# Sliding-window attention and an ELU feed-forward layer on one core: the casts on POOL in four to six instructions each instead of one

## The chip, the cores and the metric

The kernel runs on one core of one Trainium2 chip. The core has five engines that take their instructions in program order from their own queues and meet through semaphores: PE (matrix multiply, with its weight loads shown apart as PEld), DVE (vector), ACT (scalar, activation functions), POOL (GpSimd) and SP (issues transfers). SP, ACT and POOL issue DMA transfers. The metric is the time of one execution on the device in microseconds (us). The kernel before was timed seven times: median 341.12 us, lowest 340.13, highest 346.49.

## What is computed

Eight batches of eight heads, 576 positions, 64 channels per head. Each position attends to positions at most 32 away; the result of all heads (4608 tokens by 512) goes through a layer of 512 to 2048 and back with an ELU between.

```python
# _attn_ref, cut
scores = scale * np.matmul(q, k.transpose(0, 1, 3, 2))
mask = np.abs(pos[:, None] - pos[None, :]) <= 32
scores = np.where(mask, scores, -1000000000.0)
attn = softmax(scores)
attn_out = np.matmul(attn, v)              # (8, 8, 576, 64)
# _moe_ref
x = attn_out.transpose(0, 2, 1, 3).reshape(4608, 512)
h = x @ w_in                               # 512 -> 2048
g = np.where(h > 0.0, h, np.exp(np.minimum(h, 0.0)) - 1.0)
out = g @ w_out                            # 2048 -> 512
```

## The kernel before

**Inputs q and k.** They arrive as fp32 in four loads a batch: q and k, each in two halves of four heads (`load_qk`, L228), into one of four `stg` buffers. A cast (`cast`) turns each half into bf16 in a `bf` tile, of which there are four (q and k of two batches). PE then transposes the `bf` tile, one pair of heads `hp` at a time (`T`, L264 and L269), into PSUM, and ACT or DVE copies the result to `qT` or `kT` (`E`, L281 and L283).

There are two layouts. Batches 0 and 1 are "wide": 128 partitions, and a half is 2 x 576 = 1152 columns (`wide`, `TPW` = 9, `D` = 64). Batches 2 to 7 are "narrow": 96 partitions, and a half is 4 heads x 6 positions x 64 channels = 1536 columns (`HP` = 4, `TPP` = 6). Batch 0 is cast by DVE and ACT (`casts0`), batches 1 to 7 by POOL: 4 wide casts (L244) and 24 narrow ones (L252), in the order k, q, k, q, each when its load has landed.

**Attention.** For each pair `i` of blocks of 64 queries (36 pairs): scores on PE (`QK`, L327), exp on ACT (`SM`, L335) into `pu`, the mask multiplied in by two DVE instructions (`MK`, L348: `pm` = `pu` times `masks`, all three in SBUF), the product with v on PE (`AV`, L360), reciprocal and scaling on DVE (`RN`, L373 and L375) into `xs`. Then `xs` is transposed into `xt`: for the first eight pairs by PE and ACT, and for the others by a transposing transfer that SP issues (`X`, L386).

**Feed-forward.** The tokens are worked on in tiles of 256 (the first two) and 512 (the other eight). For each of 16 column groups `fo` of a tile: four matmuls into `psH` (`Hm`, L407, three buffers), exp on ACT into `e` (`EX`, L415), min(e - 1, 0) into `f`, on DVE (`FF`, L427: input `e` fp32 in SBUF, output bf16 in SBUF) or on ACT (L425), and the ELU on DVE from `psH` and `f` (`GG`, L433 or L436). The second product (`Y`, L450) runs a tile later, in parts between the `Hm` groups; ACT copies it out of PSUM (`YC`, L460) and SP stores it.

**Loads of v and of the weights.** POOL issues them (L291, L492, L497), in its queue between its casts. For batches 2 and up, SP then issues two copies that shift v by 64 partitions (`shift_v`, L298 and L300), in its queue between the stores and the transposing transfers.

**Order.** A planner written in the kernel (`Plan`) simulates the engines with an estimated duration, a rank and dependencies per operation, and issues the operations in the order of that simulation. A cast is one operation for it (`cdur`, 1.5 us on POOL, times 0.78 for a wide one). The queues are therefore fixed at build time, and a framework puts in the semaphore waits according to what each instruction reads and writes.

Of the kernel before, what the change touches and what calls it, by code (L numbers as in the profile page):

```python
# [150 lines left out]
def kernel(  # L151
# [9 lines left out]
    nc = tc.nc  # L161

    B, H, S, D = q.shape
# [7 lines left out]
    HP = H // 2  # L171
    PR = 96
    TPP = S // PR
    TPW = S // QB
# [41 lines left out]
    def wide(b):  # L216
        return b < NWB
# [13 lines left out]
    def cast(b, nm, half, eng):  # L231
        if (nm, b) not in live:
            live[nm, b] = bfp.tile(
                [128, HP, TPW, D] if wide(b) else [PR, TPP, H, D], BF16,
                name="bf", tag="bf")
        t = live[nm, b]
        if wide(b):
            src = live.pop((nm, b, half))
            dst = t[:, half * HP // 2:(half + 1) * HP // 2].rearrange(
                "p n t d -> p n (t d)")  # L240
            if eng is nc.scalar:
                nc.scalar.copy(dst, src)
            else:
                eng.tensor_copy(dst, src)  # L244
            return
        src = live.pop((nm, b, half)).rearrange("p h (t d) -> p h t d", t=TPP)
        dst = t[:, :, half * HP:(half + 1) * HP, :].rearrange(
            "p t h d -> p h t d")
        if eng is nc.scalar:
            nc.scalar.copy(dst, src)  # L250
        else:
            eng.tensor_copy(dst, src)  # L252

    def T(b, nm, hp):
        src = live[nm, b]
# [269 lines left out]
    for b in range(B):  # L525
# [4 lines left out]
        for half in range(2):  # L530
            for nm in ("q", "k"):
                deps = list(early)
                if b == 1:
                    deps.append(("SM", L1AT))
                if b == 2:
                    deps.append(("LV", 1, 8))
                if b:
                    deps.append(("C", b - 1, nm, half))
                P.op(("L", b, nm, half), "ACT" if b or nm == "q" else "SP", 0.45,
                     r0 + half, deps,  # L540
                     lambda b=b, nm=nm, half=half: load_qk(
                         b, nm, half,
                         nc.scalar if b or nm == "q" else nc.sync),
                     dma=1.6 if wide(b) else 1.85, wt=0.085, solo=0.75)
                eng = casts0[nm, half] if b == 0 else "POOL"
                deps = [("L", b, nm, half)]
                if b >= 2:
                    deps += [("T", b - 2, nm, hp) for hp in range(HP)]
                P.op(("C", b, nm, half), eng,
                     cdur[eng] * (0.78 if wide(b) else 1.0), need - 30 + half, deps,  # L550
                     lambda b=b, nm=nm, half=half, eng=eng:
                     cast(b, nm, half, engs[eng]))
# [30 lines left out]
        for hp in range(HP):  # L583
            for nm in ("q", "k"):
                n = hp * 2 + (nm == "k")
                deps = [("C", b, nm, hp // 2)]
                m = n - (4 if b == 0 else 1)
# [20 lines left out]
    for i in range(NPAIR):  # L608
# [15 lines left out]
        t, c = where[i]  # L624
# [81 lines left out]
    with tc.manual_schedule():  # L706
# [3 lines left out]
        for mi in range(3):  # L710
            m = mf[:, mi, :]
# [6 lines left out]
        for lo, key in ((0, QB), (QB, 0)):  # L718
            m = mf[lo:lo + QB, 3, :]
# [54 lines left out]
```

## Time and profile before

| what | value |
|---|---|
| median of 7 runs | 341.12 us |
| the profiled execution | 340.55 us, of which 338.8 are the span from its first to its last instruction |
| granted PE clock | full throughout |
| L427, `f` on DVE, 128x512 | 92 instructions, mean 497 ns, median 0.42 us |
| L348, mask on DVE, 128x512 | 72 instructions, mean 510 ns, median 0.418 us |
| L252, narrow cast on POOL | 24 instructions, 1.463 to 1.681 us |
| L244, wide cast on POOL | 4 instructions, 1.143 to 1.147 us |

A page of the profile gives busy time by engine, the chain of work that ended last followed back from the end, and the costliest groups of instructions with the idle time ahead of them and what ended it. The trace can be asked for a timeline of an engine in a stretch, for the chain in order of time, and for a table of busy time by stretches. All positions are in us from the start of the span. In a timeline a row gives the start, the duration, the engine, the line, the operation and the tiles, and in square brackets how long the engine was idle before and what ended that.

The 28 casts on POOL come in seven groups of four: at 26 to 37 us (wide), and at 55 to 64, 87 to 97, 115 to 125, 152 to 162, 185 to 194 and 219 to 227 us (narrow). In all groups but the first and the last, five v loads follow the fourth cast on POOL's queue without a break.

### The profile page before, as it was taken

The page shows a single profiled execution, that of the slowest core. Times are in us where ns is not written, and L with a number is a line of the kernel's source. Part 1 is how long each engine was busy: PE and PEld are TensorE (multiplying, and loading weights), DVE is VectorE, ACT ScalarE, POOL GpSimd, SP SyncE. Part 2 cuts the span into 40 slices and gives each one's busy share as a digit, 9 for nine tenths or more (in the row PEclk, how much of TensorE's full clock was granted, in tenths as well). Part 3 has the DMA queues.
Part 4 walks back from the last instruction along what each step waited for, and adds up shares of the span by engine and source line. Part 5 has one row for each costly group of instructions (what it writes and reads, how often), then busy time and mean ns, then how long its engine had stood idle before and what let it go on. Part 6 is the DMA issues. An engine that isn't in the chain of part 4 may idle for free.

```text
span 338.8 us, 7578 instructions
## 1 busy us (share of the span) xinstructions
PE 312.1 (92%) x2995; PEld 170.2 (50%) x3040; DVE 233.3 (69%) x522; ACT 207.6 (61%) x355; POOL 84.2 (25%) x96
## 2 busy tenths in 40 slices
PE   1589998799889998999999999999999999999995
PEld 1576666554444545545554555455544544444442
DVE  5778888648966796669757976697666777655500
ACT  3558868677877566655865576567655565444511
POOL 8916503800470262005501630150000000000000
PEclk9999999999999999999999999999999999999999
DMA  7999999892999889259996893684111112200021
GB/s 278 180 238 292 191 121 258 151 89 75 236 123 109 223 158 168 67 132 243 99 130 161 214 141 86 167 207 106 52 49 46 48 46 61 64 34 31 31 92 65
DMA packets 77364, 44.58 MB, mean 132 GB/s; under 512 B 54161, under 2 KB 70801, under 8 KB 77329
## 3 DMA queue, kind: packets, MB, share of 16 engines
q0 software_dynamic: 41728, 8.92, 35.0%
q1 hardware_dynamic: 24224, 17.36, 21.1%
q10 hardware_dynamic: 11376, 17.83, 20.9%
q8 instruction: 24, 0.39, 0.5%
q14 instruction: 12, 0.09, 0.1%
HBM read 36.70 MB, written 9.44 MB: 136 GB/s over the span
## 4 chain that ended last, share of the span: by engine, by line
PE 76%; DMA 8%; DVE 7%; ACT 4%; issue 2%; ACTq 1%; POOL 0%; SPq 0%; POOLq 0%
PE psH L407 32%; PE psY L450 29%; PE psO L360 4%; PE psT L269 3%; DMA stg<-in_q_dram 3%; PE psS L327 3%; DMA xt<-xs 3%; DMA stg<-in_k_dram 2%; DVE f L427 2%; DVE g L436 2%; DVE xs L375 1%; ACT e L415 1%; PE psO L450 1%; PE psS L450 1%; PE psT L450 1%
## 5 line engine op out<-in xcount | busy, mean ns | idle before, releaser
L407 PE MATMUL psH<-xt,w_in_sb 128*128 128x512 bf16 (+1 forms) x624 | 146.0, 359 | 3.6 <-DVE g L436 1.5
L415 ACT ACTIVATE e<-psH 128x512 f32<-128x512 f32 (+1 forms) x160 | 87.7, 555 | 87.2 <-PE psH L407 77.2
L450 PE MATMUL psY<-w_out_sb,g 128*128 128x512 bf16 x499 | 128.3, 379 | 2.9 <-issue 1.6
L407 PEld LDWEIGHTS <-w_in_sb 128*128 128x128 bf16 x640 | 59.1, 98 | 56.8 <-issue 4.1
L450 PEld LDWEIGHTS <-g 128*128 128x128 bf16 x576 | 52.3, 98 | 54.3 <-issue 0.9
L427 DVE TENSOR_SCALAR f<-e 128x512 bf16<-128x512 f32 (+1 forms) x108 | 54.0, 500 | 31.8 <-ACT e L415 31.7
L436 DVE TENSOR_TENSOR g<-psH,f 128x512 bf16<-128x512 f32 (+1 forms) x108 | 70.3, 651 | 3.3
L252 POOL CAST bf<-stg 96x1536 bf16<-96x1536 f32 x24 | 35.6, 1484 | 127.6 <-DMA stg<-in_k_dram 116.0
L433 DVE SCALAR_TENSOR_TENSOR g<-f,psH 128x512 bf16<-128x512 bf16 (+1 forms) x52 | 31.2, 601 | 22.2 <-ACT f L425 22.0
L335 ACT ACTIVATE pu<-psS 128x1024 bf16<-128x1024 f32 x36 | 36.8, 1023 | 4.8 <-PE psS L327 3.9
L348 DVE TENSOR_TENSOR pm<-pu,masks 128x512 bf16<-128x512 bf16 x72 | 33.7, 510 | 3.7 <-ACT pu L335 3.4
L291 POOL DMA_DIRECT2D vw<-in_v_dram x40 | 34.2, 869 | 5.1 <-DMA w_out_sb<-in_moe_w_out_dram 2.7
L360 PEld LDWEIGHTS <-pm 128*128 128x128 bf16 x576 | 26.9, 101 | 14.3 <-DVE xs L375 1.7
L375 DVE TENSOR_TENSOR xs<-psO,rc 128x256 bf16<-128x256 f32 x68 | 28.9, 424 | 2.3
L360 PE MATMUL psO<-vw,pm 128*128 128x65 bf16 x544 | 29.1, 196 | 1.3 <-DVE xs L375 0.7
L425 ACT ACTIVATE f<-e 128x512 bf16<-128x512 f32 (+1 forms) x52 | 29.4, 566 | 1.4
L373 DVE RECIPROCAL rc<-psO 128x4 f32<-128x4 f32 x68 | 12.2, 179 | 20.7 <-PE psO L360 20.0
L281 ACT COPY qT<-psT 128x576 bf16<-128x576 bf16 x30 | 19.1, 637 | 8.2 <-PE psT L269 6.5
L269 PEld LDWEIGHTS <-bf 96*128 96x128 bf16 x288 | 17.1, 98 | 11.5 <-issue 1.8
L460 ACT COPY y<-psY 128x512 f32<-128x512 f32 x33 | 18.9, 573 | 5.4 <-remote 4.3
L269 PE MATMUL psT<-ident,bf 96*128 96x96 bf16 x288 | 20.2, 206 | 1.9 <-ACT kT L281 0.8
L281 ACT COPY kT<-psT 128x576 bf16<-128x576 bf16 x28 | 17.8, 636 | 6.0 <-PE psT L269 5.4
(48 smaller groups left out, 107.4 us busy)
## 6 DMA issues: line engine op xcount, KB each, us to landing
stg<-in_q_dram ACTq DMA_DIRECT2D x16, 576.0 KB, 10.1
out_dram<-y SPq DMA_DIRECT2D x35, 256.0 KB, 3.3
stg<-in_k_dram ACTq DMA_DIRECT2D x14, 576.0 KB, 8.4
vw<-vw SPq DMA_DIRECT2D x12, 260.0 KB, 6.0
vw<-in_v_dram POOLq DMA_DIRECT2D x24, 128.0 KB, 6.5
w_in_sb<-in_moe_w_in_dram POOLq DMA_DIRECT2D x4, 512.0 KB, 9.3
w_out_sb<-in_moe_w_out_dram POOLq DMA_DIRECT2D x4, 512.0 KB, 22.3
vw<-in_v_dram POOLq DMA_DIRECT2D x16, 96.0 KB, 6.3
```

Of the source, the lines that this page charges most:

```text
L252: eng.tensor_copy(dst, src)
L269: nc.tensor.transpose(pt[:, j, :], src[:, j, 2 * hp:2 * hp + 2, :], ident[0:PR, 0:PR])
L281: nc.scalar.copy(dst, src)
L291: nc.gpsimd.dma_start(out=vt[r:r + hi - lo, qb, :, 0:D], in_=vb[lo:hi])
L335: nc.scalar.activation(pu, live.pop(("S", i)), AX.Exp, scale=SCALE)
L348: nc.vector.tensor_mul(dst, pu[:, :, s], mb)
L360: nc.tensor.matmul(o[:, j, :], lhsT=p[:, h, s * QB:s * QB + 128], rhs=vw[b % NVB][:, qb, h, :], start=(s == 0), stop=(s == 1))
L407: nc.tensor.matmul(ps, lhsT=w_in_sb[:, do, fo * 128:(fo + 1) * 128], rhs=xts[t][:, do, :], start=(do == 0), stop=(do == NDO - 1))
L415: nc.scalar.activation(e, ps, AX.Exp)
L427: nc.vector.tensor_scalar(f, e, -1.0, 0.0, ALU.add, ALU.min)
L436: nc.vector.tensor_tensor(gs[t][:, fo, :], ps, f, ALU.max)
L450: nc.tensor.matmul(ps, lhsT=gs[t][:, fo, c * 128:(c + 1) * 128], rhs=w_out_sb[:, fo, :], start=(fo == 0), stop=(fo == NFO - 1))
```

## The change

`cast` issues several instructions where it issued one. A wide cast on POOL becomes six of 128x192 (two head pairs by three column groups of 192); a narrow one becomes four of 96x384, one per head. What is read, what is written and the arithmetic stay the same.

```diff
@@ def cast @@
             if eng is nc.scalar:
                 nc.scalar.copy(dst, src)
+            elif eng is nc.gpsimd:
+                m = TPW * D // 3
+                for n in range(HP // 2):
+                    for c in range(0, TPW * D, m):
+                        eng.tensor_copy(dst[:, n, c:c + m], src[:, n, c:c + m])
             else:
                 eng.tensor_copy(dst, src)
             return
         src = live.pop((nm, b, half)).rearrange("p h (t d) -> p h t d", t=TPP)
         dst = t[:, :, half * HP:(half + 1) * HP, :].rearrange(
             "p t h d -> p h t d")
-        if eng is nc.scalar:
-            nc.scalar.copy(dst, src)
-        else:
-            eng.tensor_copy(dst, src)
+        for j in range(HP):
+            eng.tensor_copy(dst[:, j], src[:, j])
```

The planner's numbers are untouched, so no operation changes its place in any queue. On POOL the 28 casts become 4 x 6 + 24 x 4 = 120 instructions; PE, DVE, ACT and SP issue the same instructions in the same order as before. The first piece of a cast carries the wait for the load; the others have none. A transpose on PE now waits for the pieces that it reads: a narrow `T` reads two heads, so two of the four pieces, and a wide one reads three of the six, each a wait of its own.

## Prediction

> **What bounds the kernel now.** I read the page first: engine shares, then the chain that ended last, then the group of the casts.
>
> ```profile
> PE 312.1 (92%) x2995; PEld 170.2 (50%) x3040; DVE 233.3 (69%) x522; ACT 207.6 (61%) x355; POOL 84.2 (25%) x96
> PE 76%; DMA 8%; DVE 7%; ACT 4%; issue 2%; ACTq 1%; POOL 0%; SPq 0%; POOLq 0%
> L252 POOL CAST bf<-stg 96x1536 bf16<-96x1536 f32 x24 | 35.6, 1484 | 127.6 <-DMA stg<-in_k_dram 116.0 <-DMA stg<-in_q_dram 11.0 <-PE psH L407 0.6
> ```
>
> PE carries the end. POOL has almost nothing of the chain and idles 127.6 us ahead of its casts, so the length of a cast as such is not what costs. What could cost is what a cast does to another engine. The timeline of POOL and of DVE, side by side, shows it:
>
> ```profile
> 115.44 1.46 POOL L252 CAST bf<-stg 96x1536 bf16<-96x1536 f32 x1 [14.73 <-DMA stg<-in_k_dram]
> 117.75 1.46 POOL L252 CAST bf<-stg 96x1536 bf16<-96x1536 f32 x1 [0.85 <-DMA stg<-in_q_dram]
> 120.69 1.52 POOL L252 CAST bf<-stg 96x1536 bf16<-96x1536 f32 x1 [1.48 <-DMA stg<-in_k_dram]
> 123.48 1.46 POOL L252 CAST bf<-stg 96x1536 bf16<-96x1536 f32 x1 [1.27 <-DMA stg<-in_q_dram]
> ```
>
> ```profile
> 115.84 1.35 DVE L427 TENSOR_SCALAR f<-e 128x512 bf16<-128x512 f32 x1
> 118.38 1.12 DVE L427 TENSOR_SCALAR f<-e 128x512 bf16<-128x512 f32 x1
> 120.14 0.75 DVE L348 TENSOR_TENSOR pm<-pu,masks 128x512 bf16<-128x512 bf16 x2
> 121.41 1.09 DVE L427 TENSOR_SCALAR f<-e 128x512 bf16<-128x512 f32 x1
> 123.56 1.67 DVE L427 TENSOR_SCALAR f<-e 128x512 bf16<-128x512 f32 x1
> ```
>
> Columns are start and duration. L427 takes 0.42 where no cast runs. Here each one that starts inside a cast ends 0.29 after that cast ends (115.44 + 1.46 = 116.90, against 117.19), so it stood still until about 0.13 before the cast's recorded end. L348 is stretched likewise: a pair takes 0.75 alone, and 1.29, 1.56, 1.85, 1.71 and 1.71 from 88.08, 89.89, 154.03, 187.33 and 220.91. L436 and L433 never are (maxima 0.693 and 0.689). Over the run, the excess of L427 and L348 during casts sums to some 16 us of DVE time.
>
> Does it reach the end? The table by stretches (span, then busy us of PE, PEld, DVE, ACT, POOL):
>
> ```profile
> 86.00:99.00 13.00, 10.71 (x107) 5.65 (x108) 10.79 (x24) 9.68 (x16) 8.49 (x7) 1.00 0.98 170
> 114.00:132.00 18.00, 16.40 (x174) 8.83 (x176) 15.84 (x31) 11.21 (x17) 10.04 (x9) 1.00 1.17 183
> 132.00:230.00 98.00, 96.46 (x869) 50.82 (x883) 71.93 (x149) 62.95 (x105) 26.05 (x22) 1.00 0.82 150
> 230.00:330.00 100.00, 99.00 (x673) 48.14 (x683) 61.13 (x131) 53.35 (x89) 0.00 (x0) 1.00 0.18 55
> ```
>
> From 132 to 230 there are 12 casts, yet PE idles only 1.54 of 98 us. The cast-free 100 us after that show 1.00. There the DVE waits are covered by PE's own queue. Ahead of 132 it differs. In the chain in order of time, the links from 114.68 to 126.53 are all DVE, and end in a transfer that PE waits for:
>
> ```profile
> 115.92 1.28 DVE f L427
> ...
> 118.46 1.04 DVE f L427
> ...
> 123.64 1.60 DVE f L427
> ...
> 126.53 4.69 DMA xt<-xs
> ```
>
> PE's timeline gives what can be won there:
>
> ```profile
> 120.28 1.02 PE L407 MATMUL psH<-xt,w_in_sb 128*128 128x512 bf16 x4 [0.29 <-DVE g L436]
> 126.89 0.72 PE L360 MATMUL psO<-vw,pm 128*128 128x65 bf16 x8 [0.27 <-DVE pm L348]
> 129.01 0.42 PE L360 MATMUL psO<-vw,pm 128*128 128x65 bf16 x8 [0.28 <-DVE xs L375]
> 131.36 0.81 PE L407 MATMUL psH<-xt,w_in_sb 128*128 128x512 bf16 x3 [0.36 <-DMA xt<-xs]
> ```
>
> With 0.16 more at 116.00 (that gap recurs where no cast is) these are 1.36 us, of which 1.20 hang on DVE.
>
> **The change, part by part: the pieces.** 24 casts of 96x1536 become 96 of 96x384, and 4 of 128x1152 become 24 of 128x192. No such piece is in the trace. Three rows give a line: POOL's cast into masks, 256 columns, 0.396; 1152 columns, 1.146; 1536 columns, 1.463. That is 0.18 fixed and 0.837 ns a column, so 0.50 for 384 and 0.34 for 192. Independent neighbours on POOL overlap a little: the affine selects at 2.00 and 2.18 are 0.18 apart at 0.24 each, so I take 0.06 off per step. A narrow cast is then 4 x 0.44 + 0.06 = 1.82 (from 1.46), a wide one 6 x 0.28 + 0.06 = 1.74 (from 1.15). Bounds: no fixed cost at all leaves 1.46 and 1.15; 0.396 scaled by columns (0.594) or unscaled gives 2.38 for both.
>
> **What the longer casts delay.** (a) Transposes on PE (L264, L269). They wait for the pieces they read, half a narrow cast instead of all of it. In the whole trace PE waits for L252 at one place, 0.9 us at 59.49. The smallest other slack of a first transpose is that of 92.32 against a q cast ended at 90.84, 1.48 us, while half a cast is done 0.94 after its start. Cost nothing; without that cover about 0.4 at each of five batches. (b) POOL's queue behind the casts: the v loads (L291). They start 0.4 to 1.5 later. The first four casts are each followed by idle of POOL (0.87, 0.92, 1.76 and, at the ring of loads, 1.49) that absorbs 0.59 apiece. (c) SP's shift copies (L298) wait for those loads, with stores and transposing transfers queued behind. SP waited for a v load once, 0.6 us at 56.7, and the next transposing transfer starts at 70.64. Cost nothing. (d) The next batch's loads wait for the casts to free stg: the last ends at 63.88, the next load is issued at 81.79. Nothing.
>
> **What the shorter pieces free.** The disputed point is whether a waiting DVE instruction gets in between two pieces. No two casts are back to back in this trace. The nearest rows are trains of load issues on POOL, which hold DVE up as well: L427 at 127.08 took 0.59 and ended at 127.67, inside a train from 124.89 to 129.07, and the one at 99.70 took 0.49 inside 96.53 to 100.71. Both went ahead with the next POOL instruction queued. So I take "gets in", after 0.22 on average (half a 0.44 step), 0.44 at most.
>
> The Trainium skill, GPSIMD Engine Reference, section Instruction dispatch, speaks against this: consecutive Pool instructions are no barrier, and a core begins the next one once its own share is done. By it a train of pieces might never leave a hole, and the sum would be that of the second rival below, by the rows the one here; no run here shows which holds for casts.
>
> By stage:
> - 28 to 31: L427 at 29.24 took 1.09 against 0.28, behind a wide cast. It would wait 0.13, but PE's transposes at 30.23 need three pieces, ready at about the same time. Gain 0.2 of 0.60 idle.
> - 57 to 60: the q cast started at 57.97 on a landing load. Two pieces and one DVE instruction of 0.28 between them: 57.97 + 0.94 + 0.28 = 59.19 against 59.43. Gain 0.25, at most 0.5.
> - 86 to 99: excess 0.54 and 0.81 in two L348 pairs. A pair asks twice and can meet a piece each time, 0.22 + 0.44 = 0.66, so the first pair gains nothing. Of PE's idle 2.15 only 0.87 were ended by DVE or xt. Gain 0.4, between 0 and 1.35.
> - 114 to 132: the four L427 lose 0.93 + 0.70 + 0.67 + 1.25 = 3.55; with pieces 4 x 0.22 = 0.88. DVE is 2.67 earlier, more than PE can use: gain 1.2.
> - 151 to 227: 1.54 idle against 1.00 without casts, so 0.5 at most. Gain 0.2.
>
> Sum 2.25. The profiled execution took 340.55 (span 338.8 and 1.75 around it) and would take 338.3. The median of the seven, 341.12, is 0.57 above it: **338.9**. The upper bounds (0.6 + 0.5 + 1.35 + 1.36 + 0.55 = 4.36) give 336.8.
>
> **Rivals.** *Covered anyway*: what DVE gains PE does not take, because the pairs of L348 meet two pieces, instructions that missed a cast before meet a longer one now, and the four transfers xt<-xs of 4.3 to 4.7 us stay where they are. For it: PE's gaps at 87.37, 95.42 and 96.56 (0.23, 0.78, 0.27) end with ACT; against it: the all-DVE links of 114 to 126. Gain 0.2 + 0.25 + 0.3 = 0.75: 340.4.
>
> *DVE is not let in*: the pieces follow so closely that a blocked DVE instruction waits for the whole train. Each stall on the chain grows by the lengthening, 0.59 at 29.24, 0.36 at two L348 and at four L427: 0.59 + 0.72 + 1.44 = 2.75, so 343.9 (345.2 where pieces do not overlap: 0.89 + 1.08 + 2.16 = 4.1). For it: the overlapping affine selects and the rule above; against it: 99.70 and 127.08. It decides once DVE gets in at fewer than about half the boundaries (2.25 won against 2.75 lost).
>
> **How the numbers follow.** Forecast 52%, covered 23%, not let in 25%. A measurement of this kernel tells about 0.5%, 1.7 us, from no change, so faster means under 339.4. Of the forecast's 52 (own range 336.8 to 340.0) 7 lie above that: faster 45%, same 23 + 7 = 30%, slower 25%. The range reaches from the upper bounds of the gains, 336.8, into the last case, to 343.4; its rest and a few per cent below are left out.
>
> **What would show it.** Right: L427 inside casts at 0.45 to 0.9, none near 1.6; starts of pieces 0.44 apart where DVE is quiet and about 0.86 where one went between; PE idle from 114 to 132 near 0.3; L436 and L433 unchanged; PE idle from 132 to 230 about as before. Wrong: L427 still ending with the last piece, at up to 1.9 us (rival three), or short L427 and PE's gaps before 132 still there under other names (rival two). A step from piece to piece of 0.6 or more, or a wait of PE for the casts at other places than near 59.5, would break part (a).

## The result, and the profile after

The changed kernel took 338.89 us (median of 27 runs, 337.30 to 342.27) against 341.89 us for the kernel before (64 runs, taken beside it). Ratio 0.9951, 95% interval 0.9930 to 0.9972, that is 1.0 to 2.4 us less. Run again later it gave 0.9931 (0.9897 to 0.9964). The ratios leave out runs that were more than 1.5% above the fastest of their kernel, which the medians keep, so the ratio, not the 3.0 us between the two medians, is the measure, and the traces of two such runs (batches 3 and 4 split; q first with four pieces) are not used.

The page of the changed kernel, in the same three lines as before (the lines behind the casts are numbered four higher: L348 is L352, L427 is L431; the narrow cast, L252, is L256):

```profile
PE 311.2 (92%) x2995; PEld 170.1 (50%) x3040; DVE 224.2 (67%) x522; ACT 207.3 (62%) x355; POOL 101.4 (30%) x188
...
PE 81%; DMA 7%; DVE 4%; ACT 3%; issue 2%; ACTq 1%; POOL 0%; POOLq 0%
...
L256 POOL CAST bf<-stg 96x384 bf16<-96x384 f32 x96 | 49.9, 558 | 110.8 <-DMA stg<-in_k_dram 104.6
```

POOL is 17 us busier and DVE 9 us less, with the same work (second profiles of both kernels, below, have 231.1 and 225.3 us of DVE, 6 us apart). DVE's share of the chain fell from 7% to 4%. The profiled execution took 338.64 us (span 336.9). POOL and DVE in the stretch that was shown of before:

```profile
115.73 2.04 POOL L256 CAST bf<-stg 96x384 bf16<-96x384 f32 x4 [14.42 <-DMA stg<-in_k_dram]
118.11 2.29 POOL L256 CAST bf<-stg 96x384 bf16<-96x384 f32 x4 [0.33 <-DMA stg<-in_q_dram]
120.96 1.86 POOL L256 CAST bf<-stg 96x384 bf16<-96x384 f32 x4 [0.56 <-DMA stg<-in_k_dram]
123.41 2.30 POOL L256 CAST bf<-stg 96x384 bf16<-96x384 f32 x4 [0.59 <-DMA stg<-in_q_dram]
```

```profile
116.07 0.44 DVE L431 TENSOR_SCALAR f<-e 128x512 bf16<-128x512 f32 x1
...
117.89 0.42 DVE L431 TENSOR_SCALAR f<-e 128x512 bf16<-128x512 f32 x1
...
118.95 1.09 DVE L352 TENSOR_TENSOR pm<-pu,masks 128x512 bf16<-128x512 bf16 x2
...
122.63 0.47 DVE L431 TENSOR_SCALAR f<-e 128x512 bf16<-128x512 f32 x1
...
124.29 1.05 DVE L352 TENSOR_TENSOR pm<-pu,masks 128x512 bf16<-128x512 bf16 x2
125.27 0.72 DVE L431 TENSOR_SCALAR f<-e 128x512 bf16<-128x512 f32 x1
```

DVE now starts and ends in the middle of a cast: L431 at 116.07 takes 0.44 inside the cast from 115.73 to 117.77, where its counterpart took 1.35. In return the casts stretch: 1.86 undisturbed, 2.04 to 2.30 where DVE went between. The table by stretches (span, then busy us of PE, PEld, DVE, ACT, POOL) and PE's only listed gap from 114 to 132:

```profile
86.00:99.00 13.00, 10.36 (x104) 5.61 (x105) 10.58 (x25) 9.74 (x16) 10.29 (x19) 1.00 0.97 169
114.00:132.00 18.00, 17.68 (x188) 9.81 (x191) 14.26 (x33) 12.01 (x20) 12.63 (x21) 1.00 1.05 190
132.00:230.00 98.00, 96.46 (x879) 51.02 (x893) 69.11 (x153) 63.71 (x106) 33.25 (x58) 1.00 0.87 151
```

```profile
116.24 0.81 PE L454 MATMUL psY<-w_out_sb,g 128*128 128x512 bf16 x3 [0.16 <-issue]
```

The gaps that hung on DVE between 114 and 132 are gone, and so is the wait for xt at the end of that chain. From 132 to 230 PE is as busy as before to the hundredth.

A way to see where time is won: ACT issues the same 355 instructions in the same order in every kernel with this plan, so the start of the n-th one can be compared between two traces. Against the first profile of before, the changed kernel is 0.06 us late at 61 and 86 us, 0.23 late at 99, 0.24 late at 120, 1.83 early at 136 and 1.91 early from 162 on to the end. All of it seems to come from one stage. The experiments were laid out to test that. Two words in what follows: a stall is the time that a DVE instruction (f or the mask) takes beyond its usual duration because a cast is running, and PE's cover is the work that PE still has to do while DVE stalls, so that it loses nothing.

### The profile page after: what moved, and what is told of

The parts are those of the page before. It is cut to its first block, busy times and chain, and to the rows that moved or that the text cites. A ratio compares the mean times of both kernels' runs of the same rounds, so it can differ in the third digit from the quotient of the medians.

```text
span 336.9 us, 7670 instructions
## 1 busy us (share of the span) xinstructions
PE 311.2 (92%) x2995; PEld 170.1 (50%) x3040; DVE 224.2 (67%) x522; ACT 207.3 (62%) x355; POOL 101.4 (30%) x188
## 4 chain that ended last, share of the span: by engine, by line
PE 81%; DMA 7%; DVE 4%; ACT 3%; issue 2%; ACTq 1%; POOL 0%; POOLq 0%
PE psH L411 34%; PE psY L454 31%; DMA stg<-in_q_dram 6%; PE psO L364 4%; PE psT L273 4%; PE psS L331 3%; DMA xt<-xs 1%; PE psO L454 1%; PE psS L454 1%; PE psT L454 1%; PE psT L268 1%; ACT e L419 1%; ACTq L228 1%; DVE xs L379 1%; DVE g L440 1%
## 5 line engine op out<-in xcount | busy, mean ns | idle before, releaser
L256 POOL CAST bf<-stg 96x384 bf16<-96x384 f32 x96 | 49.9, 558 | 110.8 <-DMA stg<-in_k_dram 104.6
L431 DVE TENSOR_SCALAR f<-e 128x512 bf16<-128x512 f32 (+1 forms) x108 | 46.8, 433 | 32.9 <-ACT e L419 32.7
L352 DVE TENSOR_TENSOR pm<-pu,masks 128x512 bf16<-128x512 bf16 x72 | 29.9, 456 | 3.5 <-ACT pu L339 3.3
```

The lines of the kernel that those rows point to most:

```text
L256: eng.tensor_copy(dst[:, j], src[:, j])
L431: nc.vector.tensor_scalar(f, e, -1.0, 0.0, ALU.add, ALU.min)
```

## The experiments

**Only batch 4, and all but batch 4.** Edits against the changed kernel; in the first, the wide casts are whole again too:

```diff
-        for j in range(HP):
-            eng.tensor_copy(dst[:, j], src[:, j])
+        if b == 4:                 # the second: "if b != 4"
+            for j in range(HP):
+                eng.tensor_copy(dst[:, j], src[:, j])
+        else:
+            eng.tensor_copy(dst, src)
```

> Only the four casts of batch 4 (115 to 125 us) are split, in four pieces of one head each; all others, the wide ones too, are whole as before. Theory (DVE is let in between pieces, and only the stage from 114 to 132 turns this into time): DVE starts in step with the kernel before up to about 115 us, then pulls ahead by 1.9 to 2.2 us by 132 and keeps that to the end; time 1.5 to 2.2 us under the kernel before, about as fast as the changed kernel. Rival (the gain is spread over all groups of casts): a seventh of the gain, 0.3 us. Rival (the profiled difference is a luckier landing of loads): no difference.

> All casts on POOL are split as in the changed kernel, except the four of batch 4, which are whole. Theory: L-rows of f and of the mask are short everywhere but from 115 to 125 us; the start of DVE's instructions is 0 to 0.4 us ahead or behind at 100 us and no more at 132; time within 0.7 us of the kernel before. Rival (spread gain): 1.5 us under it.

Measured: 0.9963 (0.9923 to 1.0003) for batch 4 alone, 0.9920 (0.9883 to 0.9957) for all but batch 4. The first does not decide: its 1.3 us lie just under the 1.5 to 2.2 of the theory, and its interval, from none to 2.6, holds the theory and both rivals. The second misses the theory: without the split of batch 4 there should have been no gain beyond 0.7, and there is 1.5 to 4.0. The trace of the first shows something that the theory had left out. From 120 to 136 it gained 2.06 us, as expected. But from 86 to 99, where its casts are as whole as in the kernel before, it lost 2.16. POOL and DVE there:

```profile
86.61 1.46 POOL L253 CAST bf<-stg 96x1536 bf16<-96x1536 f32 x1 [19.16 <-DMA stg<-in_k_dram]
88.80 1.46 POOL L253 CAST bf<-stg 96x1536 bf16<-96x1536 f32 x1 [0.72 <-DMA stg<-in_q_dram]
91.73 1.73 POOL L253 CAST bf<-stg 96x1536 bf16<-96x1536 f32 x1 [1.47 <-DMA stg<-in_k_dram]
```

```profile
86.73 1.62 DVE L428 TENSOR_SCALAR f<-e 128x512 bf16<-128x512 f32 x1
...
89.00 1.87 DVE L349 TENSOR_TENSOR pm<-pu,masks 128x512 bf16<-128x512 bf16 x2
...
92.61 1.14 DVE L428 TENSOR_SCALAR f<-e 128x512 bf16<-128x512 f32 x1
```

In the profile before, the first cast of this group started 0.06 after an f instruction had (87.02 and 87.08), and it was the cast that took longer (1.68 in place of 1.46) and f its usual 0.42; here f starts 0.12 after the cast and waits 1.20. Whether DVE or POOL comes first decides, and the start of a cast depends on when its load lands (the brackets). The profiled execution of all but batch 4, whose stretch from 120 to 136 was 0.51 longer than before with whole casts there, took 339.90 us against a median of 338.13. So the theory was changed: a whole cast costs an amount that is drawn anew in each execution, and splitting caps it.

**Pieces that help no transpose, and two pieces.** Narrow casts only:

```diff
-        for j in range(HP):
-            eng.tensor_copy(dst[:, j], src[:, j])
+        for j in range(TPP):                       # first: 6 pieces of 256 columns
+            eng.tensor_copy(dst[:, :, j], src[:, :, j])
...
+        for j in range(0, HP, 2):                  # second: 2 pieces of 768 columns
+            eng.tensor_copy(dst[:, j:j + 2], src[:, j:j + 2])
```

> Narrow casts in six pieces of 256 columns, one position of all four heads each, so that a transpose of a pair of heads needs all six pieces; wide casts as in the changed kernel. Six pieces at 0.34 apart are about 2.1 us. Theory (the port): DVE's stalls are as short as in the changed kernel or shorter (0.34 at most per piece), time 1.3 to 2.2 us under the kernel before. Rival (the gain comes from transposes that wait for half a cast instead of all of it): the gain is gone or turned into a loss, as every first transpose waits 0.6 us longer than before; the PE wait for the casts near 59 us grows by about 0.7 us under both.

> Narrow casts in two pieces of 768 columns (two heads each, 0.82 us each by the line fitted before), which leaves the transposes' waits as fine as in the changed kernel. Theory (the port): a blocked f waits up to 0.8 us, 0.4 on average, in place of 0.22; of the 2.1 us from 114 to 132 about 1.2 to 1.8 remain; time 0.8 to 1.7 us under the kernel before. Rival (finer waits of the transposes): as fast as the changed kernel.

("The port" stands for whatever a cast on POOL and these DVE instructions cannot use at the same time; the runs show the waiting, not what lies behind it.) Measured: 0.9946 (0.9909 to 0.9983) and 0.9933 (0.9900 to 0.9966). With six pieces across the heads, each of the six transposes of a pair of heads needs one piece, and the pair is complete only after the last. At the one place where PE waits for narrow casts, near 59 us, the pair was complete 2.39 us after the cast began, later than before (1.95) and than in the changed kernel (1.44): PE waited 0.44 for the first piece, and the six transposes took 1.94 in place of 0.43. The gain is there all the same, so the finer waits of the transposes are not what pays. Two pieces do as well as four by the times: 2.3 us (0.67% of 340) in place of the 0.8 to 1.7 expected, though the interval reaches down to 1.2. Both gained 2.06 us from 120 to 136, as with four.

**Batches 3 and 4, and only the late ones.** The same edit with `b in (3, 4)` and with `b >= 5`, wide casts whole.

> Only the eight casts of batches 3 and 4 (87 to 97 and 115 to 125 us) are split in four; all others whole. Theory after the first four runs (a whole cast costs an amount that depends on where DVE's contending instructions fall: in the group at 87 to 97 us 0 in the profile before and 2.2 in that of the kernel with only batch 4 split; splitting caps it): the stage from 114 to 136 gains 2.0 to 2.1 against the kernel before, the stage from 86 to 99 lies within 0.5 of it instead of 2.2 above; time 1.5 to 2.7 us under the kernel before, no slower than the changed kernel by more than 0.5. Rival (the groups before 60 us matter as much): about half of that, 0.8 to 1.2.

> Only the twelve casts of batches 5 to 7 (after 150 us) are split; the sixteen before are whole. Theory (after 132 us PE's own queue covers what DVE loses): the stalls of f and mask after 150 us fall from up to 1.5 to 0.75 us, the start of DVE's instructions against the kernel before moves by 0.1 us at most between 140 and 240 us, time within 0.7 us of the kernel before. Rival (the gain is spread over all groups): 3/7 of it, 0.8 to 1.2 us.

Measured: 0.9970 (0.9927 to 1.0014) and 0.9999 (0.9955 to 1.0043). The late groups alone are worth nothing that these runs can tell, as expected, but the interval (1.5 us to either side) does not rule out the rival's 0.8 to 1.2. Batches 3 and 4 alone came to 1.0 us, which is the rival's figure and less than the theory's 1.5 to 2.7, though its interval reaches 2.5; so a part that matters may lie in the casts before 60 us (split in the kernel with all but batch 4, whole in this one), and the times do not settle how much.

**A cast done twice.** Against the kernel before, all casts whole:

```diff
         else:
             eng.tensor_copy(dst, src)
+            if b == 4:             # the second: "if b == 6"
+                eng.tensor_copy(dst, src)
```

> As the kernel before (all casts whole), but each cast of batch 4 is done twice over, so that POOL reads and writes for 2.9 us per cast instead of 1.46. Theory (port, with DVE let in between the two): the second whole cast stalls the next contending DVE instruction as the first did; with four more stalls of 0.5 to 1.3 us DVE is later by up to 3.5 at 126 us, and PE with it: 1.5 to 3.5 us slower than before. Rival (what counts is the delay of the transposes or of POOL's queue): the casts end 1.5 later each, their first transposes have 3.9 us of slack: no change.

> As the kernel before, but each cast of batch 6 (185 to 194 us) is done twice over. Theory (after 132 us PE's queue covers DVE's stalls): f and mask instructions stall as often again inside 185 to 198 us, the time changes by 0 to 0.6 us. Rival (the cover is nearly used up there too): 1.5 us or more slower, as with batch 4.

Measured: 1.0073 (1.0037 to 1.0109), 2.5 us slower, for batch 4, and 1.0026 (0.9988 to 1.0064) for batch 6. Longer casts of batch 4 do cost, and not by way of the transposes: PE's matmuls wait for no narrow cast in that trace. The chain there is DVE from 119.7 to 133.2 with but 0.7 us of anything else, and PE's longest gaps in that stretch end with the mask (0.92 at 130.38) and with xs (1.38 at 133.27). For batch 6 the times leave both expectations open. These are also the first casts back to back in a trace. Batch 6, POOL and DVE:

```profile
183.12 1.51 POOL L249 CAST bf<-stg 96x1536 bf16<-96x1536 f32 x1 [19.13 <-DMA stg<-in_k_dram]
184.69 1.54 POOL L251 CAST bf<-stg 96x1536 bf16<-96x1536 f32 x1
186.18 1.65 POOL L249 CAST bf<-stg 96x1536 bf16<-96x1536 f32 x1
187.90 1.54 POOL L251 CAST bf<-stg 96x1536 bf16<-96x1536 f32 x1
```

```profile
183.95 0.96 DVE L426 TENSOR_SCALAR f<-e 128x512 bf16<-128x512 f32 x1
...
185.55 2.56 DVE L347 TENSOR_TENSOR pm<-pu,masks 128x512 bf16<-128x512 bf16 x2
```

The first of the pair at 185.55 stands until the cast that ends at 186.23 is over, the second until the one that ends at 187.83 is: each waiting DVE instruction gets in at the next boundary, although POOL's next cast is ready. PE lost 1.67 us from 140 to 227 in this trace, with two gaps of 0.41 and 0.55 put down to the mask. That is the rival's figure, so the cover after 132 us is not deep.

**Both kernels again, unchanged.**

> The kernel before, unchanged, for a second profile of it. Theory (a whole cast costs an amount that depends on which DVE instructions fall into it, and that falls out anew in each execution): the excess of f and mask inside the two groups of casts near 87 and 115 us is somewhere between 1.3 and 3.6 us each, not the 1.36 and 3.55 of the first profile again; PE's gain or loss over 114 to 136 against the first profile is between 0 and -2.1 us. Rival (the cost belongs to the program's fixed order): the same two numbers within 0.3.

> The changed kernel, unchanged, for a second profile of it and more runs. Theory: the excess of f and mask is again 0.3 to 1.2 us in each group, the stage from 114 to 136 is again 2.0 to 2.1 us shorter than in the first profile of the kernel before; ratio 0.991 to 0.997. Rival (the first profile was a lucky one): stalls or the stage differ by over 0.5 us from the first profile of the changed kernel.

The second profile of before took 340.53 us, as the first (340.55), and came to it in another way: 0.32 us later than the first over 86 to 99, 2.06 earlier over 120 to 136, and 1.51 later over 140 to 227. In the stage that had looked like the whole gain it lost nothing, with whole casts. It lost the time after 150 us instead, 0.80 of the 1.51 at the group of 150 us and the rest at the two groups behind it. The first of these:

```profile
150.68 1.11 DVE L427 TENSOR_SCALAR f<-e 128x512 bf16<-128x512 f32 x1
...
152.43 2.02 DVE L348 TENSOR_TENSOR pm<-pu,masks 128x512 bf16<-128x512 bf16 x2
...
154.97 1.57 DVE L427 TENSOR_SCALAR f<-e 128x512 bf16<-128x512 f32 x1
...
159.14 1.19 DVE L427 TENSOR_SCALAR f<-e 128x512 bf16<-128x512 f32 x1
```

```profile
157.14 0.41 PE L360 MATMUL psO<-vw,pm 128*128 128x65 bf16 x8 [0.52 <-DVE xs L375]
```

These are stalls of 3.87 us in one group of casts, and a gap of PE that DVE ends. The second profile of the changed kernel agrees with its first within 0.08 us in each of the three stretches. Its stalls do not agree as well: they reach 1.50 in the group of 150 us, over the 1.2 that was expected and 0.64 over the first profile, a difference that the rival had named as its sign; the stretches come out the same nevertheless. The two profiles of before are what the theory said, in a sharper form than was expected (the late groups were not in it).

All the profiles used that keep this plan's order, worked out from their traces. The columns of excess sum, in us and good to about 0.1, by how much the f and mask instructions that overlap a group's casts exceed 0.42 (0.285 at 256 columns) and 0.415. "At 87" names the group of casts by its start. The last three columns give by how much ACT's instructions fall behind (+) or pull ahead (-) over a stretch, against the first profile of before. "w" marks a group that is whole:

| kernel | excess at 87 | at 115 | at 150, 185, 219 | 86 to 99 | 120 to 136 | 140 to 227 |
|---|---|---|---|---|---|---|
| before | 1.36 w | 3.55 w | 2.36, 2.09, 2.16 w | 0 | 0 | 0 |
| before again | 1.81 w | 1.42 w | 3.87, 2.96, 2.93 w | +0.32 | -2.06 | +1.51 |
| only batch 4 | 3.24 w | 1.34 | 1.86, 2.60, 2.81 w | +2.16 | -2.06 | +0.19 |
| all but batch 4 | 1.11 | 3.38 w | 0.91, 0.37, 0.73 | +0.22 | +0.51 | -0.08 |
| only late | 1.52 w | 1.51 w | 0.81, 0.35, 0.57 | +0.60 | -2.06 | -0.08 |
| batch 4 twice | 3.51 w | 5.12 w | 2.21, 1.72, 1.89 w | +2.96 | +2.51 | -0.02 |
| batch 6 twice | 2.55 w | 1.92 w | 1.91, 4.83, 2.17 w | +0.95 | -2.06 | +1.67 |
| changed | 1.11 | 0.97 | 0.86, 0.33, 0.76 | +0.17 | -2.06 | -0.08 |
| changed again | 1.14 | 1.26 | 1.50, 0.46, 1.22 | +0.24 | -2.06 | -0.08 |
| six across | 0.67 | 0.80 | 1.32, 1.11, 1.11 | +0.08 | -2.06 | -0.08 |
| two halves | 1.75 | 1.90 | 0.93, 1.09, 1.02 | +0.49 | -2.06 | -0.08 |

Read down a column: with pieces, each of these stretches takes its shortest time or within 0.5 of it, and the last two the same in every execution. Whole, it takes that or up to 3 us more (up to 4.6 with casts done twice). From 120 to 136 an excess of 1.9 is free and one of 3.4 to 3.6 costs 2.1 to 2.6: the cover there ends somewhere between, and what lies beyond it costs more than the difference. From 86 to 99 it covers less: 1.5 to 1.8 cost 0.3 to 0.6, 3.2 to 3.5 cost 2.2 to 3.0. Averaged over the rows (casts done twice left out), the whole groups are 0.9, 0.9 and 0.5 us later than the split ones in the three stretches, 2.35 together, from four to six profiles each; the ratios of the changed kernel, 0.9951 and 0.9931, come to 1.7 and 2.4 us.

The stretch ahead of the table is not so settled. At 86 us the profiles lie between 1.33 us earlier and 2.57 later than the first of before, with narrow casts split there (-1.33 to +1.22) as with whole ones (-0.58 to +2.57). PE's wait for the cast of q near 59 us, which hangs on a load that took from 10.2 to 11.5 us in the chains looked at, is part of it: none to 2.02 us with pieces, none to 2.17 without. That is as much as the whole gain, and splitting does not take it away.

**A try at a faster version.** In the profile of the changed kernel PE waits 1.37 us at 59.5 for the cast of q, which is loaded and cast after k though its transposes come first. Loading and casting q first from batch 2 on, with four pieces and with two:

```diff
-                     r0 + half, deps,
+                     r0 + half + 0.1 * (b > 1 and nm == "k"), deps,
...
-                     cdur[eng] * (0.78 if wide(b) else 1.0), need - 30 + half, deps,
+                     cdur[eng] * (0.78 if wide(b) else 1.0),
+                     need - 30 + half + 0.1 * (b > 1 and nm == "k"), deps,
```

> The changed kernel, with q loaded and cast ahead of k in batches 2 to 7 (a rank lower by 0.1 in the plan); the plan's order of transposes and of some other work moves with it. In the profile of the changed kernel PE waits 1.37 us at 59.5 for the cast of q, whose load was issued second and whose cast began 2.65 us after that of k. Theory (PE waits for q alone): that wait goes, 0.7 to 1.4 us less time than the changed kernel. Rival (the k transposes then wait instead, 0.5 us issue and one cast later, or the moved order costs elsewhere): within 0.5 us of the changed kernel or slower.

> As the run with q first, with narrow casts in two pieces of two heads instead of four. Theory: as with four pieces within 0.7 us, since PE takes no more of DVE's gain than two pieces give (the stage from 114 to 136 was as short with two as with four). Rival (the shorter stalls of four pieces count elsewhere): 1 us or more slower than with four.

Measured: 0.9937 (0.9897 to 0.9977) and 0.9960 (0.9915 to 1.0005); the changed kernel beside them 0.9931. No gain that can be told. PE's wait there was 0.25 us in the profile with two pieces; but with k first it had been anything from none (two halves) to 2.02 (the changed kernel again), so one profile says little, and the plan's order changed elsewhere too. Whether the wait went and was given back is left open. Two against four pieces is within the intervals. No version was found that is measurably faster than the changed kernel.

## Why the prediction was right, and where its steps were off

**The time.** 338.9 forecast, 338.89 measured; by ratio, 2.25 forecast of 340.55 (0.9934) lies within 0.9930 to 0.9972, near its fast end. The decimal agreement of the medians is luck: the medians of before moved between 341.12 and 342.28 from one set of runs to the next. The agreement of the sum is partly luck too: of its five terms none came out at its size in the first pair of profiles, and their errors cancelled (1.91 us in place of 2.25).

**DVE is let in between pieces: right, shown.** The longest f inside a cast is 0.72, from 114 to 132 as over the whole run, against 1.67, and in the run with batch 6 twice DVE went in at the boundaries of casts standing back to back. The rival "not let in" is out. L436 and L433 are unchanged, at 0.69, as forecast. Where one went between two pieces their starts are 0.51 to 0.71 apart, less than the 0.86 forecast.

**The cost of a piece: right.** Forecast 0.50 and 0.34 with steps of 0.44 and 0.28; medians 0.503 and 0.348, steps 0.45 and 0.29. An undisturbed narrow cast takes 1.86, forecast 1.82.

**What the longer casts delay, at nothing: right.** PE waits for L256 at one place only, at 59.5, as before. There the chain shows what was said of two pieces, which is the term for 57 to 60:

```profile
47.50 10.89 DMA stg<-in_q_dram
58.39 0.03 issue
58.41 0.04 POOLq L256
58.46 0.08 issue
58.54 0.96 POOL bf L256 x2
```

PE goes on 0.96 after the cast began, not 1.48. The 0.25 us forecast for this stage did not show in the pair of profiles because the load took 10.89 in place of 10.20.

**28 to 31: won more than forecast, and lost again.** Forecast 0.2; by PE's starts the changed kernel won 0.53 between 27 and 33 us, and it was 0.94 early at 58. The wait for the load of q at 59.5, 1.37 in place of 0.38, took it all back: 0.06 late at 61.

**114 to 132: mechanism right, size off.** Forecast 1.2, measured 2.06. The term was mis-sized by taking PE's listed idle (1.36) as the most that could be won. Matched one by one, PE's starts in the two traces draw apart at five places, 0.36, 0.43, 0.30, 0.44 and 0.53 us, 2.06 together. Four of them are the gaps that the prediction listed, as 0.29, 0.27, 0.28 and 0.36; the third, at 127.22, is recorded as 0.13, too short for the list. The rest, 0.07 to 0.17 at each, lies under the recorded duration of the matmul ahead, which is longer than the distance at which such matmuls start in a row: 0.38 against 0.216 for 128x512, 0.20 against 0.03 for L360.

**86 to 99: the size holds for that profile alone.** Forecast 0.4 of gain; between the two first profiles it was a loss of 0.17. DVE was 0.31 earlier there, but the transfer that PE waits for behind it took 4.86 in place of 4.31. Before and after:

```profile
98.00 1.04 PE L407 MATMUL psH<-xt,w_in_sb 128*128 128x512 bf16 x4 [0.16 <-DMA xt<-xs]
```

```profile
98.23 1.04 PE L411 MATMUL psH<-xt,w_in_sb 128*128 128x512 bf16 x4 [0.71 <-DMA xt<-xs]
```

That profile of before was also a mild draw there (1.36 of stalls; others had 1.5 to 3.5 and were up to 3.0 us later).

**After 132, "covered by PE's own queue", gain 0.2: this step failed,** though its size fits the first pair. It was read from one execution, which lost 0.08 us there. The second profile of before lost 1.59 there (+1.51 against -0.08), with stalls of 3.87, 2.96 and 2.93 in the three groups. The cover there was enough for stalls of 2.1 to 2.4 us per group, and whole casts at times exceed that.

One error lies behind the last two, and behind reading the gain of 114 to 132 as the kernel's: the sum by stages was made as if the stalls belonged to the program's order. They belong to the execution. The two profiles of before had the same total and lost it at different places. That the totals agree is chance, and so the total of the sum held while its terms did not.

## What to carry to other kernels

Where an engine stands still behind an instruction of another that is off the critical path, look at how long one such instruction is, not at how busy that engine is: shorter ones cost that engine 0.4 us or more a cast here and freed DVE of 6 to 9 us over the run. Before a gain is put down to a stage from one pair of profiles, take a second profile of the kernel before: where the start of the blocking work depends on a load's landing, the stage that loses the time may change while the total stays. Two pieces could not be told from four by the times, which fits a rule that these runs do not prove: a split needs to be no finer than brings the stalls under what the bound engine's queue covers.

## What the runs showed of the hardware that was not expected

With casts standing back to back DVE went in at each boundary, one instruction at a time: both mask instructions of a pair waited, each until the cast then running was over (2.56 for the pair at 185.55 against 0.75 alone). And a stretch of PE's work came out the same to 0.01 us (-2.06) in eight executions of seven kernels with quite different stalls on DVE (0.80 to 1.92 in that group, against 3.55 in the first profile of before), so a stall under the cover cost nothing at all there, rather than a little.
